# A planner's run-time order replaced by a table of issue order, engines and PSUM banks

## The chip, the cores and the metric

The kernel runs on one core of one Trainium2 chip. Its time is the device time of one execution in microseconds (us). Five queues of instructions work side by side and wait for each other through semaphores: TensorE (PE: matmuls; its weight loads are listed as PEld), VectorE (DVE), ScalarE (ACT), GpSimd (POOL) and SyncE (SP, which only issues DMAs here). Each executes in the order in which its instructions were written. Matmuls write into PSUM, eight banks of 128 x 2 KiB; DVE and ACT read it, POOL doesn't. A run counts as faster or slower here by the median of its times.

## The reference

Two layers follow each other. The first is an attention with a feature map of exponentials, for 8 batches, 8 heads, 576 tokens and 64 channels; the second is an MLP whose gate mixes the 576 tokens.

```python
def phi(x):                                  # x: 8, 8, 576, 64; w_phi: 64, 128
    proj = np.einsum('bhsd,df->bhsf', x, w_phi)
    proj = proj - np.max(np.abs(proj), axis=-1, keepdims=True)
    return np.concatenate([np.exp(proj), np.exp(-proj)], axis=-1)
q_p, k_p = (phi(q), phi(k))
kv = np.einsum('bhsf,bhsd->bhfd', k_p, v)
num = np.einsum('bhsf,bhfd->bhsd', q_p, kv)
den = np.einsum('bhsf,bhf->bhs', q_p, k_p.sum(axis=2))[..., None] + 1e-06
x = (num / den) with the heads side by side  # 8, 576, 512
h = np.maximum(x @ w_in, 0.0)                # w_in: 512, 1024
u, v = h[..., :512], h[..., 512:]
v_n = (v - mean(v)) / np.sqrt(var(v) + 1e-06)
v_s = np.einsum('ts,bsd->btd', w_spatial, v_n) + b_spatial[None, :, None]
out = (u * v_s) @ w_out                      # 8, 576, 512, float32
```

## The kernel before

**Tiles.** Of each batch's 576 tokens 512 are the main part (128 partitions, each with 4 tokens) and 64 are the tail; the tails of two batches share the 128 partitions. Attention works on *units*: a pair of heads of one batch (32 of them) or the tails of two batches with all heads (4). Main matmul operands are bf16, sums are float32 in PSUM.

**A unit** takes these steps, each an operation of the plan: q and k are transposed (early on PE with a copy out of PSUM, L630 and L636, from batch 2 on by a DMA transpose, L650); k is projected (L692); DVE takes the largest absolute value (`mk`, L719), ACT the two exponentials (`kf`, L728), and of the negated maxima (`em`, L735); POOL scales v by them (`vs`, L745 and L750). For q the maximum (`mq`, L795) is split into two bf16 parts (`mhl`, L806 and L811; on DVE for the first `EARLY` units, later on POOL), transposed by PE (L818), copied (`mT`, L824) and subtracted inside the projection (L834 and L839) before the exponentials (`qf`, L850). Then come the products with v (L899 and L902), their copy (`kv`, L911), the numerator (L927; tails L986), its division (L870 and L874 on DVE, into `x`), and the transpose of `x` for the MLP: a DMA transpose (L945) from unit `XX` on, PE with a copy before (L956, L962).

**The MLP of a batch**: four V products (L1031) with their ReLU into `vr` (L1020 or L1022), their mean and variance on DVE (L1046, L1048), the inverse root on POOL (`root`, L1057 to L1059), the normalized rows `vn` (L1064, POOL or DVE); four U products (L1158) with a ReLU into `uT`; four spatial products S (L1208, L1210) that DVE multiplies into `uT` (L1217); four output products O (L1101), each copied from PSUM to `ob` (L1106, ACT or DVE) and stored by SP (L1109). Tails take the same steps with half-size tiles (L1184, L1228, L1230, L1239).

**Constants.** `w_spatial` lies in a `vn` slot until PE has transposed it into `w_spT`, in six blocks of 576 columns. The last two hold the tail's 64 rows of either batch, with the bias as one more row. For them `f_bias` copies the tail columns and the bias into zeroed tiles `wspr` and `wsptr` (L576 to L579, eight copies), which PE transposes (L599, L600); L603 copies each block out of PSUM. All six block transposes wait for `f_bias`.

**What sets the order.** The kernel first lists its operations by calls of `add`: name, engines that may run it with a cost on each, what it depends on, a priority (a due time), buffers and PSUM banks that it takes. `Plan.order` then plays a schedule through with these costs: at each step the engine that can start first takes the ready operation of the earliest due time, an operation that two engines may do goes to the one that ends it first, banks are given out as they come free, and gaps of PE are filled with dummy matmuls (`keep_busy`, L402) up to a certain time. The operations are emitted in the order of the planned starts, and each engine keeps it. `SLOTS` has the number of buffers of each kind, `OFF`, `MLP` and `TUNE` the due times. A buffer kind with n slots goes round: the (n+1)-th use waits for the first one's readers.

Of the kernel before, what the change touches and what calls it, by code (L numbers as in the profile page):

```python
# [15 lines left out]
SLOTS = dict(kh=2, qh=3, vh=2, tl=1, kT=3, qT=7, kTb=1, qTb=3, kf=4, kft=2, qf=3, qft=2, vs=2, kv=3, x=3, xt=5,  # L16
             xT=3, xTt=3, vn=4, uT=2, uTt=1, vr=6, ob=7, mk=5, mq=2, em=3, emt=4, p0=4, mhl=1, mT=2)
OFF = dict(load=-24.36, T=-3.87, KP=-4.21, KM=0.82, KE=-8.23, EM=0.69, VS=-1.33, QP=0.79, QM=-5.85, MH=-0.05,
           MT=-3.88, FP=7.29, FE=8.25, KV=5.67, NU=8.31, XT=10.0)
PERIOD = 5.47  # L20
MLP = dict(at0=6.87, step0=1.63, at1=14.14, step1=1.44, at2=11.57, step2=1.84, at3=6.46, step3=1.72, at4=25.75,
           step4=0.83, at5=6.71, step5=1.58, at6=23.42, step6=0.25, at7=-1.6, step7=5.16)
TUNE = dict(lq=3.79, w0=-3.66, w1=-2.36, w2=6.25, w3=10.12, l8=-6.73, l9=4.4, l10=0.1, l11=-7.8, l13=0.92,
            tq=-2.75, tk=-9.53, vt0=4.02, vt1=-0.82, u8=-2.33, u9=3.32, u10=7.42, u11=0.12, u12=1.18, u13=0.32,
            u14=0.0, u15=0.76, u16=1.44, u17=0.87, u18=0.31, u19=-3.88, u20=-2.72, u21=-1.32, u22=-0.19, u23=0.75,
            u24=0.04, u25=-0.04, u26=1.88, u27=-4.23, u28=1.49, u29=-0.34, u30=-3.18, u31=-1.7, u32=-1.2, u33=1.1,
            u34=0.77, u35=1.94, v0=0.75, bsp=-10.97, WT=26.11, wsp=9.28, wstep=2.27, vload=-1.26, cross=30.56,
            KC=1.58, u0=0.3, u1=3.71, u2=5.78, u3=-5.24, u4=1.74, u5=-11.18, u6=4.58, u7=-2.79, l0=-3.51, l1=2.4,
            l2=-1.13, l3=-2.83, l4=3.99, l5=2.31, l6=11.26, l7=-3.04, T0=-20.55, XTp=15.35, TN=-1.21)
# [4 lines left out]
WARM = 62.86  # L34
WARM0 = 22.63
FILL = 0.54
EARLY = 10
TCA = 14
VG0 = -1
VG1 = 1  # L40
VG2 = 2
VG3 = 2
VGT = -1
XB = 2
XX = 7
# [4 lines left out]
LONE = 0.0  # L50
# [10 lines left out]
class Op:  # L61
    __slots__ = ("engs", "emit", "deps", "left", "nexts", "allocs", "uses", "prio", "mode", "work", "ready", "done",
                 "name", "eng", "start", "follow", "after", "banks", "gates", "last")
# [11 lines left out]
class Plan:  # L75
# [28 lines left out]
    def order(self):  # L104
        lanes = {"SW": [], "HW": []}

        def lane(e):
            return lanes["SW" if e == "POOL" else "HW"]

        free = dict.fromkeys(self.ENGS, 0.0)  # L110
        pools = {k: [0.0] * n for k, n in SLOTS.items()}
        banks = [0.0] * BANKS
        held = float("inf")

        def place(n, t):

            fit = [i for i in range(BANKS - n + 1) if max(banks[i:i + n]) <= t]
            if n == 1:
                return max(fit, key=lambda i: (banks[i ^ 1] == held, banks[i]))
            return max(fit, key=lambda i: (i % 2 == 0, min(banks[i:i + n])))  # L120
        cand = {e: [] for e in self.ENGS}
        mode, server, out = 0, 0.0, []

        def release(op):
            op.after = {e: max([op.ready] + [d.done + (OWN if d.eng == e else WAKE) for d in op.deps]) for e in op.engs}
            for e in op.engs:
                cand[e].append(op)

        for op in self.ops:
            if op.left == 0:  # L130
                release(op)

        def earliest(op, e):
            t = max(free[e], op.after[e])
            need = {}
            if op.banks:
                n = len(op.banks)
                t = max(t, min(max(banks[i:i + n]) for i in range(BANKS - n + 1)))
                if t == held:
                    return None  # L140
            for b in op.allocs:
                need[b.pool] = need.get(b.pool, 0) + 1
            for p, n in need.items():
                if len(pools[p]) < n:
                    return None
                t = max(t, heapq.nsmallest(n, pools[p])[-1])
            for b in op.uses:
                if b.at is not None and b.who not in (None, e):
                    t = max(t, b.end + WAKE)
            if op.work is not None and len(lane(e)) >= 8:  # L150
                t = max(t, lane(e)[-8])
            if e == "PE" and op.mode != mode:
                t = max(t, free[e] + SWITCH)
            return t

        todo = len(self.ops)
        while todo:
            best = None
            for e in self.ENGS:
                if not cand[e]:  # L160
                    continue
                est = [(t, op) for op in cand[e] if (t := earliest(op, e)) is not None]
                if not est:
                    continue
                t0 = min(t for t, _ in est)
                if best is None or t0 < best[0]:
                    best = (t0, e, est)
            if best is None:
                raise RuntimeError("stuck: " + ", ".join(f"{o.name}" for e in self.ENGS for o in cand[e])[:800])
            t0, e, est = best  # L170
            slack = SWITCH + 1 if e == "PE" else 1
            est = [(t, op) for t, op in est if t <= t0 + slack]
            ready = [op.mode for _, op in est]

            def rank(op):
                if e != "PE" or op.mode == mode:
                    return op.prio
                return op.prio + GROUP + (LONE if op.mode == 1 and ready.count(1) < 2 else 0)
            pick = min((rank(op), k, t, op) for k, (t, op) in enumerate(est))
            _, _, t, op = pick  # L180
            if len(op.engs) > 1:
                fin = {}
                for f in op.engs:
                    tf = earliest(op, f)
                    fin[f] = tf + op.engs[f][1] + BIAS.get(f, 0)
                g = min(fin, key=fin.get)
                if g != e:
                    e, t = g, earliest(op, g)
            cost, lat = op.engs[e]
            for f in op.engs:  # L190
                cand[f].remove(op)
            op.eng, op.start = e, t
            if e == "PE" and self.filler is not None and self.filler[0].done is not None:
                a = max(free["PE"], self.filler[0].done + WAKE) + (SWITCH if mode else 0.0)
                z = t - (SWITCH if op.mode else 0.0)
                pace = 55.6 if a > 1e3 * WARM0 else 106.7
                n = int((z - a) * (1.0 if a < 1e3 * WARM0 else FILL) / pace)
                fit = [i for i in range(BANKS) if banks[i] <= a]
                if n >= 3 and a < 1e3 * WARM and fit:
# [5 lines left out]
            if e == "PE":  # L205
                mode = op.mode
# [1097 lines left out]
```

## Time and profile before

| | us |
|---|---|
| median of three runs | 268.99 (267.04 to 269.32) |
| the profiled execution | 265.37 |
| its span, first to last instruction | 263.6 |
| PE busy, with its waits inside a pipelined run | 243.6 |
| DVE, ACT, POOL busy | 212.2, 205.8, 181.6 |

The durations below come from the profiled execution. In a line of a group the numbers after the bar are the group's busy time, the mean of one in ns, and the idle time before it with what ended it. A stretch lists the busy time of PE, PEld, DVE, ACT and POOL in it, then the granted clock of PE, the DMA share and GB/s. In the chain a row has its start, its length and what it was. A DMA's landing is told from its issue. Matmuls overlap, so a row of one is longer than the distance to the next.

### The profile page before, as it was taken

To read this page: it belongs to the slowest core of one execution; us is meant where nothing else is said; L and a number is where in the kernel's file an instruction comes from. 1 tells how busy PE (TensorE), PEld (TensorE's weight loads), DVE (VectorE), ACT (ScalarE), POOL (GpSimd) and SP (SyncE) were. 2 spreads that over 40 slices of the span, in tenths; PEclk is the share of its full clock that TensorE was granted. 3 is DMA by queue.
4 is the path that set the end of the run, shared out by engine and by line. 5 is a ranking of instruction groups with operands and counts; after the bars stand their busy time and mean duration, and the time that the engine had idled before them with its cause. 6 is when DMAs were issued, how large, how long until landed. Compare 5 with 4: busy or idle time off the path is not lost.

```text
span 263.6 us, 8301 instructions
## 1 busy us (share of the span) xinstructions
PE 243.6 (92%) x3331; PEld 151.1 (57%) x3331; DVE 212.2 (81%) x406; ACT 205.8 (78%) x341; POOL 181.6 (69%) x306
## 2 busy tenths in 40 slices
PE   6777879999999999989999999969999999999993
PEld 5555666665656656555565775535676665545451
DVE  6899999989988999898999988857988973646610
ACT  5899898879898959869989886938988887665043
POOL 8798949769997889668999958548997440173000
PEclk9999999999999999999999999999999999999999
DMA  7999996999599999998989999999754038320036
GB/s 140 209 235 202 229 210 69 230 162 130 51 211 211 228 161 198 181 280 83 185 108 169 160 166 178 211 276 232 125 122 82 16 28 211 112 80 1 0 116 246
DMA packets 85047, 41.12 MB, mean 156 GB/s; under 512 B 53968, under 2 KB 80272, under 8 KB 85008
## 3 DMA queue, kind: packets, MB, share of 16 engines
q1 hardware_dynamic: 58288, 29.14, 56.9%
q0 software_dynamic: 26640, 11.41, 36.2%
q8 instruction: 26, 0.43, 0.8%
q14 instruction: 13, 0.11, 0.1%
q10 hardware_dynamic: 80, 0.03, 0.0%
HBM read 32.85 MB, written 9.44 MB: 160 GB/s over the span
## 4 chain that ended last, share of the span: by engine, by line
PE 65%; DMA 14%; DVE 7%; POOL 5%; ACT 4%; issue 3%; DVEq 0%; ACTq 0%; POOLq 0%
PE banks L1101 11%; PE banks L1208 10%; PE banks L1158 9%; PE banks L1031 9%; DMA qh<-in_q_dram 7%; DMA w_in<-in_moe_w_in_dram 5%; PE banks L899 5%; PE banks L927 4%; PE banks L692 4%; PE banks L834 2%; PE banks L1210 2%; DMA kTb<-kh 2%; PE banks L839 2%; POOL vs L750 2%; DVE x L874 2%
## 5 line engine op out<-in xcount | busy, mean ns | idle before, releaser
L850 ACT ACTIVATE qf<-banks 128x1024 bf16<-128x1024 f32 x64 | 64.3, 1032 | 8.4 <-PE banks L839 8.4
L728 ACT ACTIVATE kf<-banks 128x1024 bf16<-128x1024 f32 (+1 forms) x66 | 65.6, 1010 | 4.6 <-PE banks L692 2.6
L750 POOL TENSOR_TENSOR vs<-vh,em 128x512 bf16<-128x512 f32 x64 | 65.5, 1044 | 0.5
L719 DVE TENSOR_REDUCE mk<-banks 128x8 f32<-128x1024 f32 x36 | 43.7, 1216 | 6.0 <-PE banks L692 4.6
L795 DVE TENSOR_REDUCE mq<-banks 128x8 f32<-128x1024 f32 x26 | 31.4, 1218 | 5.3 <-PE banks L692 4.3
L1208 PE MATMUL banks<-w_spT,vn 128*128 128x512 bf16 x128 | 32.9, 379 | 0.7 <-DVE x L874 0.7
L1031 PE MATMUL banks<-w_in,xT 128*128 128x512 bf16 x128 | 31.6, 379 | 0.0
L1101 PE MATMUL banks<-w_out,uT 128*128 128x512 bf16 x128 | 31.1, 379 | 0.0
L1106 ACT COPY ob<-banks 128x512 f32<-128x512 f32 (+1 forms) x28 | 16.4, 588 | 18.7 <-PE banks L1101 18.6
L1158 PE MATMUL banks<-xT,w_in 128*128 128x512 bf16 x128 | 31.0, 379 | 0.0
L1046 DVE BATCH_NORM_STATS2 stats<-vr 128x6 f32<-128x512 bf16 (+1 forms) x37 | 25.1, 680 | 5.3 <-ACT vr L1022 5.1
L899 PE MATMUL banks<-vs,kf 128*128 128x66 bf16 x512 | 24.7, 193 | 1.5 <-POOL vs L750 0.9
L1217 DVE TENSOR_TENSOR uT<-banks,uT 128x512 bf16<-128x512 f32 x32 | 21.6, 684 | 4.5 <-PE banks L1210 4.0
L899 PEld LDWEIGHTS <-kf 128*128 128x128 bf16 x512 | 21.8, 97 | 5.3 <-issue 1.9
L874 DVE TENSOR_TENSOR x<-banks,rc 128x512 bf16<-128x512 f32 x32 | 22.0, 688 | 0.7
L1064 POOL TENSOR_SCALAR vn<-vr,rs 128x512 bf16<-128x512 bf16 x29 | 22.2, 779 | 0.4
L1022 ACT ACTIVATE uT<-banks 128x512 bf16<-128x512 f32 x25 | 14.9, 603 | 8.6 <-PE banks L1158 8.6
L927 PEld LDWEIGHTS <-qf 128*128 128x128 bf16 x512 | 19.3, 97 | 4.1 <-issue 0.5
L927 PE MATMUL banks<-kv,qf 128*128 128x66 bf16 x512 | 21.2, 193 | 0.5 <-ACT kv L911 0.3
L902 PE MATMUL banks<-vst,kft 128*128 128x66 bf16 x128 | 21.1, 192 | 0.0
L1022 ACT ACTIVATE vr<-banks 128x512 bf16<-128x512 f32 x25 | 15.0, 605 | 5.9 <-PE banks L1031 5.3
L1208 PEld LDWEIGHTS <-vn 128*128 128x128 bf16 x128 | 11.6, 97 | 13.1 <-issue 0.3
(131 smaller groups left out, 490.0 us busy)
## 6 DMA issues: line engine op xcount, KB each, us to landing
out_dram<-ob SPq DMA_DIRECT2D x32, 256.0 KB, 3.5
vh<-in_v_dram SPq DMA_DIRECT2D x14, 512.0 KB, 6.6
kh<-in_k_dram POOLq DMA_DIRECT2D x15, 256.0 KB, 5.8
qh<-in_q_dram POOLq DMA_DIRECT2D x15, 256.0 KB, 7.8
vh<-in_v_dram SPq DMA_DIRECT2D x4, 256.0 KB, 8.1
v_tl<-in_v_dram SPq DMA_DIRECT2D x8, 128.0 KB, 7.3
w_in<-in_moe_w_in_dram POOLq DMA_DIRECT2D x2, 512.0 KB, 14.5
out_dram<-ob SPq DMA_DIRECT2D x8, 128.0 KB, 2.7
```

The source lines that it names most:

```text
L719: nc.vector.tensor_reduce(out=mk.t[:, cols(rs)], in_=heads(ck, rs), axis=AX.X, op=ALU.max, apply_absolute_value=True)
L728: nc.scalar.activation(out=kfc.t[:, s, cols(rs), :], in_=heads(ck, rs), func=AF.Exp, bias=0.0, scale=sc)
L750: nc.gpsimd.tensor_tensor(out=vs.t[:, s, :, 0:D].rearrange("p (r x) d -> p r x d", r=2), in0=vc.t[:, lo:lo + H, :].rearrange("p (x r) d -> ...
L795: nc.vector.tensor_reduce(out=mq.t[:, cols(rs)], in_=heads(cq, rs), axis=AX.X, op=ALU.max, apply_absolute_value=True)
L850: nc.scalar.activation(out=qc.t[:, s, cols(rs)], in_=cf.t[:, rs].rearrange("p r (x t) -> p (r x) t", t=P), func=AF.Exp, bias=0.0, scale=sc)
L899: nc.tensor.matmul(out=pv[:, hh, s, :], lhsT=u["kf"].t[:, s, j, :], rhs=u["vs"].t[:, s, j, :], start=(n == 0), stop=False)
L927: nc.tensor.matmul(out=pn[:, hh, pos * DA:(pos + 1) * DA], lhsT=u["qf"].t[:, s, 4 * (pos // 2) + 2 * hh + pos % 2, :], rhs=kv["c"].t[:, 2 ...
L1022: nc.scalar.activation(out=out_, in_=in_, func=AF.Relu, bias=0.0, scale=1.0)
L1031: nc.tensor.matmul(out=pv[r], lhsT=lhs(kc), rhs=w_in_bf[:, kc, HALF:DFF], start=(kc == 0), stop=(kc == KC - 1))
L1101: nc.tensor.matmul(out=po[r], lhsT=lhs(dc), rhs=w_out_bf[:, dc, :], start=(dc == 0), stop=(dc == KC - 1))
L1158: nc.tensor.matmul(out=pu, lhsT=w_in_bf[:, kc, dc * P:(dc + 1) * P], rhs=xT["c"].t[:, kc, :], start=(kc == 0), stop=(kc == KC - 1))
L1208: nc.tensor.matmul(out=ps, lhsT=VN[bb]["c"].t[:, sp, cs], rhs=w_spT[:, sp, 0:T0], start=(sp == 0), stop=False)
```

## The change

1. `Plan.order` no longer plans. It reads `ORDER`, a string of 1514 words. A number is the place of an operation in the list of `add` calls; a letter behind it is the engine (P, A, D, G, S for PE, ACT, DVE, POOL, SP) where more than one is allowed; the number behind a colon is the first PSUM bank. `w0x17` is 17 dummy matmuls into bank 0; there are 11 such words with 86 in all. The operations are emitted in the order of the words.
2. `SLOTS` changes: more of `qh`, `qTb`, `x`, `xT`, `mk`, `mq`, `em`, `emt`, `mT`; fewer of `qf`, `xTt`, `vn`, `ob`, `p0`. `EARLY` goes from 10 to 12, `TCA` (units whose transposed copies ACT may do) from 14 to 11, `XX` from 7 to 6. DMA transposes of q and k begin with the same unit as before.
3. `root` writes into the mean-and-variance tile itself: the variance plus 1e-6, then its power -0.5; the third operation (the negated mean) goes, and the normalization subtracts the mean and multiplies in place of adding and multiplying.
4. `wspr`, `wsptr` and their memsets go. `f_bias` only casts the bias to bf16, two copies on ACT. PE transposes the tail columns and the bias columns straight from where they were loaded, each of the last two blocks in ten transposes in place of five, and only these two wait for `f_bias`. The last block is copied out in two parts; the rows between are zeroed by one memset of `w_spT`'s last two blocks.
5. The last output block is copied in two halves of 256 columns, the first by ACT and stored from ACT's queue, the second by DVE and stored by SP.

```diff
+        out = []
+        for word in ORDER.split():
+            if word[0] == "w":
+                i, n = map(int, word[1:].split("x"))
+                op = Op("warm", {"PE": (n * 55.6, n * 55.6 + 164)}, lambda e, i=i, n=n: self.filler[1](i, n), 0.0)
...
+                head, _, bank = word.partition(":")
+                op = self.ops[int(head.rstrip("PADGS"))]
+                op.eng = dict(zip("PADGS", self.ENGS)).get(head[-1]) or next(iter(op.engs))
                 for k, b in enumerate(op.banks):
+                    b.at = int(bank) + k
             out.append(op)
...
+ORDER = """
+21 2 18 8D 3 9D 0 19 72 24 73 27 16 20 14 17 w0x17 117:2 11G 4 118D w0x4 125:6 23 5 6 7 189:4 22 26 126D 119:2
...
+1462 1469:4 1464 1471:1 1470 1477:6 1472 1480:4 1478D 1467:2 1479 1481D 1376 1370 1486:4 1468 1482 1465:3 1487A
+1488 1483:7 1466 1473:6 1484A 1485 1489:2 1474A 1476 1492:3 1490A 1475 1495:0 1491 1493A 1494 1498:6 1496A 1497
+1499 1500 1501 1502
+"""
...
     def f_bias(e):
         copy = nc.vector.tensor_copy if e == "DVE" else nc.scalar.copy
-        for bl, col in ((0, TL), (1, 0)):
-            copy(out=wspr[:, :, bl, bl * D:bl * D + TL], in_=wspc.t[:, :, T0:S])
-            copy(out=wsptr[:, bl, bl * D:bl * D + TL], in_=wspt[:, T0:S])
-            copy(out=wspr[:, :, bl, col:col + 1], in_=bsp.unsqueeze(2))
-            copy(out=wsptr[:, bl, col:col + 1], in_=bspt)
+        copy(out=bspb[:, 0:NB], in_=bsp)
+        copy(out=bspb[:TL, NB:NB + 1], in_=bspt)
...
+            r, rb = slice(bl * TL, (bl + 1) * TL), slice(TL - bl * TL, TL - bl * TL + 1)
+            for rr, main, tail in ((r, lambda cc: wspc.t[:, cc, T0:S], wspt[:, T0:S]),
+                                   (rb, lambda cc: bspb[:, cc:cc + 1], bspb[:TL, NB:NB + 1])):
                 for tp, cc in enumerate(POS):
+                    nc.tensor.transpose(out=pt[rr, tp * P:(tp + 1) * P], in_=main(cc), identity=ident)
+                nc.tensor.transpose(out=pt[rr, T0:S], in_=tail, identity=ident[:TL, :TL])
...
-            nc.gpsimd.tensor_scalar(out=var[r, 0:n], in0=m[r, 0:n, 1:2], scalar1=1e-6, scalar2=None, op0=ALU.add)
-            nc.gpsimd.tensor_scalar(out=rs[r, 0:n, 1:2], in0=m[r, 0:n, 0:1], scalar1=-1.0, scalar2=None, op0=ALU.mult)
-            nc.gpsimd.tensor_tensor(out=rs[r, 0:n, 0:1], in0=var[r, 0:n], in1=neghalf[r, 0:n].unsqueeze(2), op=ALU.pow)
+            d["rs"] = m = mv()
+            nc.gpsimd.tensor_scalar(out=m[r, 0:n, 1:2], in0=m[r, 0:n, 1:2], scalar1=1e-6, scalar2=None, op0=ALU.add)
+            nc.gpsimd.tensor_tensor(out=m[r, 0:n, 1:2], in0=m[r, 0:n, 1:2], in1=neghalf[r, 0:n].unsqueeze(2), op=ALU.pow)
...
+        if last:
+            h = DM // 2
+            for n, (e_, c, dma, cost) in enumerate((("ACT", act(h), nc.scalar, 600.0), ("DVE", dve(h), nc.sync, 480.0))):
+                cs = slice(n * h, (n + 1) * h)
...
+                    (nc.vector.tensor_copy if e == "DVE" else nc.scalar.copy)(out=ob.t[r, cs], in_=pc.t[r, cs])
...
+                    add("OD", {"ACT" if n == 0 else "SP": (cost, 0)}, lambda e, dst=dst, rr=rr, cs=cs, dma=dma: dma.dma_start(
+                        out=dst[:, cs], in_=ob.t[rr, cs]), prio - 20, deps=[o2], uses=bufs(ob), work=(900, 128 * 55 / 16))
```

The table was read by numbering the `add` calls. Against the order before, output blocks copied whole by DVE go from 9 to 16 (by ACT from 28 to 20), copies of transposed q and k on DVE from 18 to 21, one of the four `vst` memsets goes to POOL, and SP's first DMA is the first k load in place of `w_phi`. On POOL's queue the loads of q and k of batch 0 and of batch 1's first four heads stand ahead of all weights, and `w_in` stands behind those of batch 1's other heads.

## The prediction

> **What bounds the kernel now.** I read the busy shares first, then the stretches of 10 us, then the chain, the waits and the timeline around what the change touches.
>
> ```profile
> PE 243.6 (92%) x3331; PEld 151.1 (57%) x3331; DVE 212.2 (81%) x406; ACT 205.8 (78%) x341; POOL 181.6 (69%) x306
> ```
>
> TensorE (PE) looks full, but a busy PE may be a waiting one. So I also counted from the start of each matmul to the start of the next. Back to back, a 128x512 matmul takes 0.216 us in this trace (four in 0.86 in the chain), one of 128 columns 0.056, one of 66 columns 0.03. What exceeds that is stall: 38.5 us in all, 17.0 of it before 40 us, 2.4 from 40 to 50, 16.7 from 50 to 180, and 2.4 after that. A further 4.7 us went to 85 filler matmuls (L402), all before 26 us. So there are 43 us to win at the very most, and over half of that lies in the first 50.
>
> ```profile
> 10.00:20.00 10.00, 7.39 (x134) 5.56 (x134) 9.55 (x21) 9.28 (x17) 8.73 (x12) 1.00 1.29 230
> 20.00:30.00 10.00, 7.64 (x165) 5.89 (x160) 9.25 (x25) 8.52 (x16) 8.95 (x13) 1.00 1.26 212
> 40.00:50.00 10.00, 9.42 (x161) 6.48 (x160) 9.87 (x23) 8.47 (x17) 9.71 (x14) 1.00 0.87 146
> ...
> 200.00:210.00 10.00, 10.00 (x153) 6.34 (x152) 9.08 (x16) 7.76 (x14) 4.49 (x10) 1.00 0.22 42
> ```
>
> Columns: PE, PEld, DVE, ACT, POOL busy, clock, DMA, GB/s. From 10 to 60 us VectorE (DVE) is busy for 47.1 of 50 us while PE stalls: DVE paces the start. From 180 on PE runs without stall, so the end is the time at which that stretch begins, plus fixed work. The chain names another suspect for the start, the loads:
>
> ```profile
> 7.39 13.05 DMA w_in<-in_moe_w_in_dram
> 20.72 17.49 DMA qh<-in_q_dram
> ```
>
> The second half of `w_in` and other weights stand in the queue ahead of batch 1's q and k; that q load was issued at 20.7 and landed at 38.2. PE itself shows only 0.8 us of idle for it, so I count DVE as the limit and the loads as close behind.
>
> **The change part by part**, against this execution's own 265.4 us (span 263.6 and 1.8 around it). That is 3.6 below the 269.0 median of the other runs; I carry the difference over.
>
> *Bias block.* The eight copies of `f_bias` stand in DVE's queue at the worst place:
>
> ```profile
> 25.26 1.03 DVE L577 COPY wsptr<-wspt 64x64 bf16<-64x64 bf16 x1
> ...
> 27.54 0.14 DVE L806 CAST mhl<-banks 128x8 bf16<-128x8 f32 x1
> 27.72 0.17 DVE L811 TENSOR_TENSOR mhl<-banks,mhl 128x8 bf16<-128x8 f32 x1
> ```
>
> ```profile
> 27.94 0.38 PE L630 MATMUL banks<-ident,kh 128*128 128x128 bf16 x4 [1.01 <-DVE mhl L811]
> ```
>
> They run from 24.95 to 27.62, 2.7 us, and PE is idle for 1.0 behind them. After the change two small ScalarE copies replace them (0.2 to 0.3 each, by the small rows 0.226 of `em` and 0.292 of `wphi`). Added: a memset of 1152 bf16 per partition, about 0.55 by the `wspr` row (0.485 for 512 words), in place of 0.65, both in DVE's idle first 5 us; one more eviction into `w_spT`, 0.44; and ten more PE transposes, 20 against 10, at 0.056: +0.6 on PE.
>
> *DVE's queue.* I added row means for what stands ahead of the numerator product (L874) in the old order and in the table. Ahead of batch 0's last pair it is 40.6 us before and 35.9 after; of batch 1's, 61.9 and 57.4; of batch 4's, 151.8 and 147.5; of batch 5's, 173.1 and 170.3; of batch 7's, 218.7 and 218.2. Neighbours overlap (all rows sum to 233.5, the busy time is 212.2), so 4.5 is 4.1 of real time. This holds the bias block, three more transposed copies on DVE (0.42 each), two more units whose maxima are split on DVE (four ops of 0.154, taken from POOL), and some work put later. The table also gives seven more whole output copies to DVE (16 against 9, 0.69 each), most of them late, where DVE is half idle. With DVE 94% busy up to 60 us, at most 4.1 is gained and at least 0, if its waits for data grow instead; I take **-3.0**, nearer to the top because the busy share is near one.
>
> *Order of loads.* SP's first load, k, moves ahead of `w_phi`: issue at 0.72 in place of 1.36, **-0.6**, since the first cast and transpose wait for it (the trace has 0.8 of DVE idle there). On POOL's queue q and k of batch 0 and of batch 1's first four heads go ahead of all weights, those of its other heads ahead of `w_in`, and the first half of `w_in` moves from the 10th place to the 32nd, behind 16 DMA issues (8 before) and 13 value products and casts. Nearest rows: PE idle for q and k loads 0.8 and 0.6. I take **-0.8**; the ends are the losing rival below (+7.9) and the winning one (-8).
>
> *Table and buffers from 50 us on.* The PE work of the MLP that stands ahead of each pair's numerator differs by at most 3 us up to batch 5 (54.6 and 54.6 at pair 2 of batch 4), so the mixture is the old one. What differs is detail: banks, neighbours, engines, more `mT`, `mq`, `em`, `x` and `xT` slots, fewer `qf` and `ob`. PE's idle time behind the maxima chain (L818 and L630 waiting for `mhl`) is 4.2 us in all, 1.0 of it the bias block's. I take a third of the rest, **-1.0**; the ends are a loss of 3 and a gain of 4 (a quarter of the 16.7).
>
> *One more unit transposed by DMA:* four PE transposes fewer, -0.2, against +0.6 above: **+0.4**.
>
> *Root in two GpSimd ops:* `rs` L1058 goes, 0.24 times 13 on POOL. In the last batch it stands on the way to `vn`, but PE is busy with other products there (10.00 of 10 from 230 to 250): 0. Were that cover gone, 0.2.
>
> *Last block in two halves.* Now: copy 0.58, then issue at 259.86 and landing at 262.29. A half is 0.39 on ScalarE or 0.42 on DVE by the `kv` rows of 264 columns. Side by side they would win 0.16. But both read one bank, and this trace shows two engines waiting for each other over a bank without sharing data:
>
> ```profile
> DVE mk L719 <- ACT kf L728: 0.5, 2, 0.3
> ```
>
> ```profile
> ACT kf L728 <- DVE mk L719: 1.4, 3, 0.6
> ```
>
> So one half after the other: 0.81, +0.2; half the bytes may return 0.1: **+0.1**. The Trainium skill (PSUM — Partial Sum Buffer, "PSUM bank collisions raise a hardware error") says that two engines reading one bank and quadrant at once is an error even at different columns, and has it guarded by a semaphore; it speaks against this edit, and the two waits agree. Without that rule the edit would be -0.2.
>
> Sum: -3.0 -0.6 -0.8 -1.0 +0.4 +0.1 = **-4.9**: 260.5 for a profiled execution, **264** as a median. A stall that goes from the start isn't lost later, since PE's work from 180 us on stays in order and without gaps: after the last pair's numerator the table leaves 30 us of PE work where the old order leaves 34. DVE and PE are late next, together.
>
> **Rivals.**
> 1. *The weights come late (slower).* Ahead of the first half of `w_in` on POOL now stand 16 DMA issues of 0.75 us (12.0), 8 value products of 1.05 and 5 casts of 0.21 (9.4) and some 1.5 of setup, and POOL idled 3.4 in its first 20 us: issue at about 26 in place of 7.4. At 13 to 18 us to landing, as here, that is 39 to 44, and the first product that needs it starts at 39.6 now: a stall of 0 to 4.5. The other half follows some 7 us later, landing at 46 to 51; the first U product, which the table puts about 6 us earlier than today's 53.6, waits 0 to 3.4 more. Together up to +7.9, less the 4.9 won elsewhere: +3, **272**. It decides from a landing after about 44.5, 4.9 beyond today's start of that product. Against it: less is queued ahead when q and k of batch 1 are through early. Chance 0.13, other losses of a fixed order included.
> 2. *Nothing much changes.* DVE's earlier work only moves its waits; PE's stalls from 50 to 180 stay, and the extra output copies sit in DVE's way. Bias block's 1.0 and the first load's 0.6, less 0.5: about -1, **268**. Chance 0.17; this is also what is left if the table reproduces the old order in effect.
> 3. *The loads were the limit.* The chain holds 30 us of DMA before 38 us. If q and k of batch 1, no longer queued behind `w_in` and `w_out`, let PE fill half of the 17 us of stall before 40: -8, plus -1 each of table and bias: about -10, **259**. For it: the chain; against it: DVE's 94%. Chance 0.24.
>
> My forecast has the remaining 0.46. The range goes from 257.5, which leaves out the upper part of the third rival (0.07), to 270.5, which leaves out most of the first and the rim of the second (0.14): with that 0.79 is inside. About 1% is what a measurement of this kernel can tell from no change (266.3 to 271.7). Faster: 0.46 and 0.24 make 0.70; same 0.17; slower 0.13.
>
> **What would show it.** No `wsptr` rows on DVE, and no PE idle on `mhl` near 28 us. PE stall before 50 us down from 19.4 to about 15, the fillers about the same 86. DVE still above 9.2 of 10 from 10 to 60 us; if it falls below 8.5 while PE gains, the third rival holds. The first V product (L1031) near 36 us; a wait of it on DMA `w_in` means the first. PE from 180 on without stall. In the last 5 us an ACT and a DVE copy of 256 columns one after the other. I am wrong if stall between 50 and 180 us grows by more than 4, or if gains come from there and not from the start.

## The result and the profile after

| | before | after |
|---|---|---|
| median | 268.01 us (264.78 to 269.32, four runs) | 307.8 us (306.57 to 308.57, four runs) |
| ratio, 95% interval | | 1.157 (1.146 to 1.168) |
| the profiled execution, its span | 265.37, 263.6 | 308.57, 306.8 |

The ratios and their intervals, here and below, leave out the runs that took over 1.5% longer than the fastest of the same kernel; medians and ranges are of all runs.

The forecast was 264. The kernel is 16% slower, 37 us beyond the upper end of the range. The answers to the views shown of before follow. First the busy time of each engine over the span, then the chain's shares by engine, both from the page of after:

```profile
PE 251.7 (82%) x3301; PEld 155.3 (51%) x3338; DVE 216.9 (71%) x411; ACT 199.2 (65%) x332; POOL 229.1 (75%) x291
...
PE 37%; POOL 32%; DMA 10%; DVE 10%; issue 6%; ACT 1%; POOLq 1%; SPq 1%; DVEq 0%; ACTq 0%
```

PE isn't busy for 55.1 us (306.8 less 251.7), where it was 20.0 before: 35.1 of the 43.2 us that the span grew. The other 8.1 are busy time of PE: matmul rows are longer on average (S, 0.413 us in place of 0.379), and the granted clock is below 1.00 in many stretches now. GpSimd (POOL) has 47.5 us more work with 15 instructions fewer, and from 5% of the chain it came to 32%.

The stretches of after (columns: PE, PEld, DVE, ACT, POOL busy, clock, DMA, GB/s):

```profile
10.00:20.00 10.00, 8.13 (x142) 6.84 (x139) 9.07 (x20) 9.66 (x20) 7.16 (x12) 1.00 1.20 187
20.00:30.00 10.00, 6.48 (x115) 5.36 (x114) 5.85 (x15) 6.11 (x12) 6.12 (x8) 0.83 0.46 63
...
60.00:70.00 10.00, 5.28 (x77) 2.98 (x75) 7.06 (x12) 8.71 (x17) 9.68 (x8) 0.94 1.30 155
...
100.00:110.00 10.00, 5.41 (x94) 3.62 (x94) 5.65 (x9) 7.41 (x12) 9.63 (x8) 0.99 0.90 171
...
230.00:240.00 10.00, 3.75 (x33) 1.89 (x33) 3.94 (x5) 4.23 (x7) 9.89 (x10) 0.81 0.29 68
```

In three of them POOL is full, with 8 to 10 instructions in 10 us, while PE works for 3.8 to 5.4. In each of them a batch's four rows `vn` are normalized. What PE waited for (us in all, times, the longest):

```profile
PE banks L1174 <- POOL vn L1015: 12.1, 7, 4.6
PE banks L771 <- POOL mhl L764: 9.7, 3, 6.2
PE banks L852 <- POOL vs L703: 7.5, 5, 3.4
PE banks L855 <- POOL vst L728: 3.5, 1, 3.5
```

All listed waits of PE that POOL ended make 38.5 us, against 3.3 before. The second and third row are not the normalization itself but what stands behind it on POOL: the split maxima `mhl` and the scaled v, both of the attention. POOL's groups name the operation (busy, mean ns of one, idle before):

```profile
L1015 POOL TENSOR_SCALAR vn<-vr,mv 128x512 bf16<-128x512 bf16 x30 | 62.2, 2080 | 0.6
L1015 POOL TENSOR_SCALAR vnt<-vr,mv_t 64x512 bf16<-64x512 bf16 x7 | 14.6, 2084 | 0.6
...
L1015 DVE TENSOR_SCALAR vn<-vr,mv 128x512 bf16<-128x512 bf16 x2 | 0.8, 408 | 0.3 <-POOL mv L1010 0.3
```

The same group on POOL before:

```profile
L1064 POOL TENSOR_SCALAR vn<-vr,rs 128x512 bf16<-128x512 bf16 x29 | 22.2, 779 | 0.4
```

One normalization on POOL takes 2.08 us in place of 0.78, on the same tile with the same types: 37 of them (36 before) at 1.30 more are 48.1 us; POOL's busy time grew by 47.5. On DVE the same line still takes 0.41. The timeline of POOL in after shows what that does to its queue (start, duration):

```profile
101.95 8.26 POOL L1015 TENSOR_SCALAR vn<-vr,mv 128x512 bf16<-128x512 bf16 x4
110.16 0.19 POOL L759 CAST mhl<-mq 128x8 bf16<-128x8 f32 x1
110.43 0.20 POOL L764 TENSOR_TENSOR mhl<-mq,mhl 128x8 bf16<-128x8 f32 x1
```

Two ops of 0.2 us for the next unit's maximum stand behind 8.26 us of normalization. Here PE waited for `vn` itself (3.1 and 1.5 us). PE's longest wait for `mhl` comes at a later batch, where one of the two small ops stands behind the fourth row (POOL's timeline, then PE's):

```profile
237.55 2.07 POOL L1015 TENSOR_SCALAR vn<-vr,mv 128x512 bf16<-128x512 bf16 x1
239.59 0.20 POOL L764 TENSOR_TENSOR mhl<-mq,mhl 128x8 bf16<-128x8 f32 x1
```

```profile
239.85 0.29 PE L771 MATMUL banks<-ident,mhl 128*128 128x128 bf16 x1 [6.20 <-POOL mhl L764]
```

In the last microseconds of after the two halves of the last block stand one after the other (the number in brackets is the idle time before):

```profile
301.97 0.37 ACT L1063 COPY ob<-banks 128x256 f32<-128x256 f32 x1 [0.28 <-PE banks L1052]
...
302.38 0.42 DVE L1063 COPY ob<-banks 128x256 f32<-128x256 f32 x1 [4.94 <-ACT ob L1063]
```

### The profile page after: what moved, and what is told of

Read it like the earlier page. It is cut to its first block, busy times and chain, and to the rows that moved or that the text cites. A ratio compares the mean times of both kernels' runs of the same rounds, so it can differ in the third digit from the quotient of the medians.

```text
span 306.8 us, 8238 instructions
## 1 busy us (share of the span) xinstructions
PE 251.7 (82%) x3301; PEld 155.3 (51%) x3338; DVE 216.9 (71%) x411; ACT 199.2 (65%) x332; POOL 229.1 (75%) x291
## 4 chain that ended last, share of the span: by engine, by line
PE 37%; POOL 32%; DMA 10%; DVE 10%; issue 6%; ACT 1%; POOLq 1%; SPq 1%; DVEq 0%; ACTq 0%
POOL vn L1015 16%; PE banks L1052 8%; PE banks L1174 6%; POOL vs L703 6%; PE banks L984 5%; DMA v_tl<-in_v_dram 4%; POOL vnt L1015 3%; PE banks L645 3%; DMA kTb<-kh 3%; PE banks L1124 3%; DVE stats L999 2%; POOL mv L1010 2%; PE banks L880 2%; PE banks L852 2%; DMA vh<-in_v_dram 2%
## 5 line engine op out<-in xcount | busy, mean ns | idle before, releaser
L803 ACT ACTIVATE qf<-banks 128x1024 bf16<-128x1024 f32 x64 | 62.6, 1028 | 20.8 <-PE banks L792 17.7
L681 ACT ACTIVATE kf<-banks 128x1024 bf16<-128x1024 f32 (+1 forms) x66 | 64.1, 1005 | 13.9 <-DVE mk L672 7.8
L1015 POOL TENSOR_SCALAR vn<-vr,mv 128x512 bf16<-128x512 bf16 x30 | 62.2, 2080 | 0.6
L1174 PE MATMUL banks<-w_spT,vn 128*128 128x512 bf16 x122 | 36.9, 413 | 12.4 <-POOL vn L1015 12.1
L672 DVE TENSOR_REDUCE mk<-banks 128x8 f32<-128x1024 f32 x36 | 43.5, 1216 | 4.5 <-PE banks L645 3.9
L748 DVE TENSOR_REDUCE mq<-banks 128x8 f32<-128x1024 f32 x24 | 29.1, 1214 | 6.0 <-PE banks L645 5.9
L984 PE MATMUL banks<-w_in,xT 128*128 128x512 bf16 x118 | 29.8, 379 | 0.9 <-DVE ob L1072 0.2
L1072 ACT COPY ob<-banks 128x512 f32<-128x512 f32 (+1 forms) x20 | 11.7, 588 | 20.0 <-PE banks L1052 19.5
L880 PE MATMUL banks<-kv,qf 128*128 128x66 bf16 x512 | 22.3, 198 | 0.0
L698 POOL CAST vs<-em 128x32 bf16<-128x32 f32 x32 | 6.8, 215 | 19.3 <-PE banks L984 10.1
L864 ACT CAST kv<-banks 128x264 bf16<-128x264 f32 x25 | 9.6, 383 | 15.6 <-PE banks L855 14.7
```

Source lines behind the costliest of these rows:

```text
L672: nc.vector.tensor_reduce(out=mk.t[:, cols(rs)], in_=heads(ck, rs), axis=AX.X, op=ALU.max, apply_absolute_value=True)
L681: nc.scalar.activation(out=kfc.t[:, s, cols(rs), :], in_=heads(ck, rs), func=AF.Exp, bias=0.0, scale=sc)
L803: nc.scalar.activation(out=qc.t[:, s, cols(rs)], in_=cf.t[:, rs].rearrange("p r (x t) -> p (r x) t", t=P), func=AF.Exp, bias=0.0, scale=sc)
L880: nc.tensor.matmul(out=pn[:, hh, pos * DA:(pos + 1) * DA], lhsT=u["qf"].t[:, s, 4 * (pos // 2) + 2 * hh + pos % 2, :], rhs=kv["c"].t[:, 2 ...
L984: nc.tensor.matmul(out=pv[r], lhsT=lhs(kc), rhs=w_in_bf[:, kc, HALF:DFF], start=(kc == 0), stop=(kc == KC - 1))
L1015: (nc.vector if e == "DVE" else nc.gpsimd).tensor_scalar(out=dst, in0=src, scalar1=rs[:, 0:1], scalar2=rs[:, 1:2], op0=ALU.subtract, op1=A ...
```

## The experiments

Three theories stood at first. **Theory 1**: the normalization that subtracts costs more on POOL, and that alone makes the loss. **Theory 2**: the table itself is at fault (its order, fewer `vn` slots), and the long rows are its by-product. **Theory 3**: the place of the operands is at fault, since mean and root now lie in the tile that DVE wrote. Times are medians. The experiments ran in three groups, each on a chip of its own, and the kernel before was run beside them each time: 269.11 (19 runs), 268.71 (29) and 268.17 (17). Lines of the table in the diffs are cut out of its text.

### The ALU operation alone

The kernel after with one word changed. The mean is added in place of subtracted, so this kernel leaves out the mean's sign.

```diff
-                                                               op0=ALU.subtract, op1=ALU.mult)
+                                                               op0=ALU.add, op1=ALU.mult)
```

> The changed kernel with one word altered: the normalization adds the mean in place of subtracting it (so its output isn't the reference's: the sign of the mean is wrong). Theory 1: on GpSimd a tensor_scalar with subtract and mult takes 2.08 us where one with add and mult took 0.78, 37 times, and POOL's extra 48 us make the loss. Then the rows return to about 0.78 and the time falls to 258 to 266. Theory 2: the table itself is at fault (its order, fewer vn slots), the long rows are its by-product: the time stays above 295. Theory 3: the operands' place is at fault (mean and root now lie in the tile that DVE wrote): rows stay near 2.08 and the time near 308.

Measured: 270.39 (265.4 to 272.11), 0.993 of before (0.985 to 1.000). The line's own view in this kernel (shortest, median, longest in ns; first and last start in us):

```profile
L1015 POOL TENSOR_SCALAR vn<-vr,mv x30: 757/766/899, 61.9 to 250.5; 128x512 bf16<-128x512 bf16 x30
```

Same order, same buffers, same operands, same places in the queue: 0.77 again, and 37 us are back. Theories 2 and 3 fall for the loss. The time is above the 258 to 266 that I expected: the loss is gone, and hardly a gain is left. The waits of PE that POOL ended fall from 38.5 to 7.2 us.

### The old root within the table

The kernel after with the three-op root and the normalization that multiplies and adds as before; it is also the base for what follows.

```diff
-            d["rs"] = m = mv()
-            nc.gpsimd.tensor_scalar(out=m[r, 0:n, 1:2], in0=m[r, 0:n, 1:2], scalar1=1e-6, scalar2=None, op0=ALU.add)
...
+            nc.gpsimd.tensor_scalar(out=rs[r, 0:n, 1:2], in0=m[r, 0:n, 0:1], scalar1=-1.0, scalar2=None, op0=ALU.mult)
...
-                                                               op0=ALU.subtract, op1=ALU.mult)
+                                                               op0=ALU.add, op1=ALU.mult)
```

> The changed kernel with the old root and normalization put back (three GpSimd ops, add and mult), all else as changed. Theory 1: within 1% of the run that only adds, since the third op is 0.24 us on POOL 13 times; 258 to 267, and against the kernel before the 4.9 us faster that I summed, if the rest of my working holds. Theory 2: above 295. Theory 3: 258 to 267 as well.

Measured: 268.95 (266.51 to 271.77), 0.999 of before (0.993 to 1.004). So all the rest of the change, which I had put at -4.9, comes out at nothing. The third op costs 13 times 0.24 on POOL, and nothing can be seen of it in the time: the kernel with two ops and an addition isn't distinguishable from this one.

### The new root in the old kernel

The kernel before with only the two-op root and the subtracting normalization; the planner plays its schedule through anew with the costs that the change gives (1400 in place of 1720 for a root).

```diff
-            nc.gpsimd.tensor_scalar(out=rs[r, 0:n, 1:2], in0=m[r, 0:n, 0:1], scalar1=-1.0, scalar2=None, op0=ALU.mult)
...
-                                                               op0=ALU.add, op1=ALU.mult)
+                                                               op0=ALU.subtract, op1=ALU.mult)
```

> The kernel before with only the new root and normalization (two ops, subtract and mult); its planner still counts 0.74 us for a normalization. Theory 1: rows of 2.08 us, POOL some 45 us busier, and 295 to 315 us. Theory 2: within 1% of the kernel before. Theory 3: as theory 1.

Measured: 321.71 (316.21 to 323.79, four runs), 47 to 55 more than before. The line's view:

```profile
L1062 POOL TENSOR_SCALAR vn<-vr,mv x29: 2062/2066/2216, 58.0 to 298.2; 128x512 bf16<-128x512 bf16 x29
```

It takes neither the table nor any other part of the change to get the slow rows, and the loss is greater here than with the table. The 36 rows account for 47 us of POOL's time; what makes the rest (the planner's new order, or a lower clock: 0.935 as a mean in the profile) was not taken apart.

### The subtraction in the second place

Is it the subtraction, or its place as the first of two operations? This kernel (on the best one below) multiplies first, then subtracts the mean times the root; that product is a third small op on POOL.

```diff
+            nc.gpsimd.tensor_tensor(out=m[r, 0:n, 0:1], in0=m[r, 0:n, 0:1], in1=m[r, 0:n, 1:2], op=ALU.mult)
...
-                                                               op0=ALU.add, op1=ALU.mult)
+                                                               op0=ALU.mult, op1=ALU.subtract)
```

> The table with both sets of moves, the normalization written as value times root, minus mean times root (mult, then subtract), the product of mean and root as a third GpSimd op. If any subtract makes the GpSimd tensor_scalar slow, its rows are near 2.08 us and the time is above 295; if only a subtract in the first place does, the rows are near 0.78 and the time is 263 to 267.

Measured: 308.22 (307.8 to 308.64, two runs), 1.152 of before (1.143 to 1.161), and 43 more than the same kernel with the old root and the addition (265.11 in this group).

```profile
L1013 POOL TENSOR_SCALAR vn<-vr,mv 128x512 bf16<-128x512 bf16 x30 | 62.1, 2074 | 0.6
```

2.07 in either place. So it is the subtraction on POOL. Why it is slow there, no run shows.

### Where the -4.9 went: the bias block

With the loss explained, the open question was why the rest gives nothing. First, the bias block put back into the kernel with the old root: eight copies on DVE at the bias's place in the table, five transposes per block, and the two memsets.

```diff
-        copy(out=bspb[:, 0:NB], in_=bsp)
-        copy(out=bspb[:TL, NB:NB + 1], in_=bspt)
-    i_bias = add("bias", {"ACT": (196, 340)}, f_bias, WT + 4, [l_bsp, l_bspt])
+        for bl, col in ((0, TL), (1, 0)):
+            copy(out=wspr[:, :, bl, bl * D:bl * D + TL], in_=wspc.t[:, :, T0:S])
...
+    i_bias = add("bias", {"DVE": (900, 980)}, f_bias, WT + 4,
...
```

> As the run with the old root and normalization in the table, and the bias block put back too: zeroed copies made by eight DVE copies in the place of the table's bias word, five PE transposes for each of the two blocks. If the bias block is worth what I summed (up to 2.7 us of DVE in the paced stretch, of 3.0), this is 1.5 to 3 us slower than that run; if DVE has slack in the table's start, it is within 1.

Measured: 272.41 (269.59 to 276.6), 1.011 of before (1.000 to 1.021). That is 3.4 more than the 268.95 without it, though with these spreads anything from about 0 to 6 would fit. And the trace doesn't put it on the block. In the table the eight copies stand at 48.1 us, not at 25, and take 0.8 us together, not 2.7. The copies of `wsptr` (kernel before, then this one):

```profile
L577 DVE COPY wsptr<-wspt x2: 1015/1022/1028, 25.3 to 26.5; 64x64 bf16<-64x64 bf16 x2
...
L534 DVE COPY wsptr<-wspt x2: 163/164/165, 48.3 to 48.7; 64x64 bf16<-64x64 bf16 x2
```

DVE's row just ahead of them starts at 47.01, where the same row of the base kernel starts at 44.68: 2.3 us of the difference are there before the first copy. The row behind them is 3.1 late, the next of its kind 2.1. In the profiles PE waits 5.3 us for `kTb` and 3.5 for `vst` in place of 4.2 and 3.0, and those are loads and transposes that the block doesn't touch. What the block's change is worth in the table this run doesn't show; its own work there is 0.8 us of DVE, besides the memsets at the start.

### A queue that stands on one load

In the kernel with the old root PE idles twice for 3 us, on `vst`, where it did not before, and on `kTb`, where it waited 2.3 before. The first is in its weakest stretch:

```profile
20.00:30.00 10.00, 7.12 (x105) 5.89 (x106) 5.33 (x16) 5.57 (x11) 7.23 (x11) 0.66 0.59 91
```

DVE works 5.33 of 10 here, where it worked 9.25 before. POOL's timeline shows where that starts:

```profile
11.35 0.21 POOL L698 CAST vs<-em 128x32 bf16<-128x32 f32 x1 [0.28 <-ACT em L688]
14.53 1.04 POOL L703 TENSOR_TENSOR vs<-vh,em 128x512 bf16<-128x512 f32 x1 [2.97 <-DMA vh<-in_v_dram]
```

The table lets POOL scale the *second* pair's v ahead of the first's. The second v load was issued at 8.20 and landed at 14.45; the first pair's v had landed at 7.54 and stood in line behind it. The tail's v, which the table loads after that on SP (issued at 9.32 where it was 3.97, landed at 19.88 where it was 12.07), comes last of all, and PE waits for its product (PE's timeline):

```profile
22.89 0.21 PE L855 MATMUL banks<-vst,kft 128*128 128x66 bf16 x1 [3.02 <-POOL vst L728]
```

In the next kernel five words of the start are moved: on SP the tail's v loads ahead of the second v load, on POOL the first pair's products ahead of the second's and batch 0's tail ahead of batch 1's, on PE one projection of k ahead of a transpose.

```diff
-w0x4 125:6 23 5 6 7 189:4 22 26 126D 119:2 190 74 229:6 25 120A 75 76 230 w0x3 199:2 191 77 31
+w0x4 23 5 6 7 189:4 125:6 22 26 126D 119:2 190 74 229:6 120A 75 76 230 w0x3 199:2 191 77 25 31
...
-131:3 196 232 202
+131:3 196 198 197 232 202
...
-211 w6x6 237:5 214 198 205 206:2 238 212 217 197 w7x3 133:7 207 136D w6x4 129:1 134D 216 239 240
+211 w6x6 237:5 214 205 206:2 238 212 217 w7x3 133:7 207 136D w6x4 129:1 134D 216 215 239 240
...
-248 241:4 215 221
+248 241:4 221
```

> The table with the old root and normalization (269.0), and five words of the start moved: on POOL the two v products of the first pair go ahead of those of the second, and the two v products of batch 0's tail ahead of batch 1's; on SP the two v tail loads go ahead of the second v load, which waits for a transpose; on PE the first k projection goes ahead of the third k transpose. Theory A: what the table loses is head-of-line waiting in its start (POOL idle 3.0 us before its first v product, PE idle 3.0 us on the tail's, DVE busy only 5.3 of 10 us from 20 to 30): then the hole at 20 to 23 us closes and it is 3 to 4 us faster than that run, 265 to 266. Theory B: the start is slack, since PE has MLP work to catch up with later: within 1 us.

Measured: 267.16 (264.27 to 268.94), 0.991 of before (0.987 to 0.995). The stretch:

```profile
20.00:30.00 10.00, 8.14 (x165) 6.67 (x163) 9.38 (x24) 9.36 (x15) 7.66 (x11) 1.00 0.86 151
```

DVE is at 9.38, PE at 8.14 and the clock at 1.00; the 3 us on `vst` are gone. Over 20 to 40 us DVE works 18.5 of 20; in four profiles with the old start (the base kernel, the last block whole, two slots for `kTb`, the addition) it works 14.3 to 15.8. The time falls by 1.8, less than the 3 to 4 expected. The 3.0 was a long case: PE's wait on `vst` is 3.0, 2.2, 1.3 and 1.3 us in those four profiles.

### A transpose that waits for its only buffer

The second idle spell, from the waits and the timeline of the kernel with the old root (two views):

```profile
PE banks L645 <- DMA kTb<-kh: 4.2, 2, 3.0
```

```profile
72.95 0.60 PE L645 MATMUL banks<-wphi,kTb 64*128 64x128 bf16 x8 [2.99 <-DMA kTb<-kh]
```

`kTb`, the target of k's DMA transposes, has one slot. The projections that read its former content start at 62.48, the next transpose into it was issued at 63.81, and it landed 9.1 us later. The next kernel gives it two, and moves that transpose (the second of batch 2) up behind the one before it on SP.

```diff
-SLOTS = dict(kh=2, qh=4, vh=2, tl=1, kT=3, qT=7, kTb=1, qTb=4,
+SLOTS = dict(kh=2, qh=4, vh=2, tl=1, kT=3, qT=7, kTb=2, qTb=4,
...
-1034 160 339:6
+1034 160 159 339:6
...
-371 159 1059:1
+371 1059:1
```

> The table with the old root and normalization, a second kTb slot, and the DMA transpose of k for batch 2's second half moved ahead in SP's queue. In the run without it, it is issued at 63.8 after the readers of the one slot, lands at 72.9, and PE idles 3.0 us for it. Theory A (single waits at the table's fixed order cost what they last): 2.5 to 3.5 us faster, 265.5 to 266.5. Theory B: within 1 us, a later wait takes its place (DMA queues are the most loaded there).

Measured: 267.28 (263.89 to 268.89), 0.993 of before (0.988 to 0.997). The transpose is now issued at 55.5, and PE's wait for `kTb` falls to 1.3 us:

```profile
PE banks L642 <- DMA kTb<-kh: 1.3, 1, 1.3
```

### Both

> Both sets of moves. Theory A: the two add up, 262 to 263.5, 2% faster than the kernel before. Theory B: 266 to 269.

> The table with both sets of moves once more, on the chip of these runs, to compare the first two with: 262.5 to 266, about 1.5% faster than the kernel before.

The second is the same kernel once more, on the chip of the third group. Measured: 264.56 (262.49 to 265.2), 0.985 of before (0.979 to 0.990), and 265.11 (262.18 to 267.79), 0.987 (0.978 to 0.995). The two sets of moves add up within the spread: 1.8 and 1.7 apart, 4.4 and 3.8 together against 268.95. The base kernel ran on another chip; by the ratios to before, which allow for that, it is 2.0 and 1.6 apart, 3.8 and 3.2 together, each with about 2 to either side. Stretches of the first:

```profile
20.00:30.00 10.00, 8.46 (x174) 7.13 (x169) 9.42 (x21) 9.30 (x15) 6.42 (x10) 1.00 0.81 154
...
70.00:80.00 10.00, 9.35 (x154) 5.93 (x152) 9.79 (x18) 9.53 (x16) 6.98 (x10) 1.00 1.30 162
```

Where PE worked 7.12 and 6.62 in these two stretches of the base kernel, it works 8.46 and 9.35. This is the fastest kernel here, 1.3 to 1.5% better than the one before.

### Three edits that were asked for by a doubt

**The last block whole.** The base kernel with the last block copied by ACT and stored by SP, as the other blocks are.

```diff
-1499 1500 1501 1502
+1499 1500
...
-                       bufs(UT[bb]["c"]), [(dst, slice(0, P))], last=bb == B - 1 and j == NB - 1)
+                       bufs(UT[bb]["c"]), [(dst, slice(0, P))], last=False)
```

> The table with the old root and normalization, the last output block copied whole by ScalarE and stored by SP, as before the change. From the last matmul's end to the span's end it was 4.4 us in the kernel before and 4.9 with the halves, one after the other on their bank; I had 0.1. So the tail row: 4.4 to 4.5; the time 0 to 0.5 us below the run with halves, which a median can't tell.

Measured: 268.44 (265.8 to 273.5) against 268.95: no difference. From the last matmul's end to the end of the span it is 4.8 us whole and 4.9 in halves. The whole copy:

```profile
260.99 0.58 ACT L1074 COPY ob<-banks 128x512 f32<-128x512 f32 x1 [0.28 <-PE banks L1054]
```

0.58 here, and 0.37 and 0.42 with 0.03 between them in halves: a copy longer by 0.24, which half as much to store does not win back.

**More dummy matmuls.** The granted clock was 0.66 from 10 to 20 us in one profile of the fastest kernel, so its 86 dummies were doubled (`w0x17` to `w0x34` and so on).

```diff
-21 2 18 8D 3 9D 0 19 72 24 73 27 16 20 14 17 w0x17 117:2 11G 4 118D w0x4 23
+21 2 18 8D 3 9D 0 19 72 24 73 27 16 20 14 17 w0x34 117:2 11G 4 118D w0x8 23
```

> The table with both sets of moves and twice the dummy matmuls in each of the eleven words (172 in place of 86). The profile of the run without has a granted clock of 0.66 from 10 to 20 us, the kernel before had 1.00 there. Theory A: the clock costs time at the start: the share returns to 1.00 and it is 1 to 2 us faster. Theory B: DVE and the loads pace the start, so PE's clock is covered: within 1 us, or up to 2 slower where the dummies delay a transpose.

Measured: 267.55 (264.53 to 272.54), 0.998 of before, 2.4 slower than the same kernel without them in the same group. The other profile of that kernel, without extra dummies, has the clock at 1.00 there:

```profile
10.00:20.00 10.00, 8.07 (x147) 7.04 (x148) 9.07 (x20) 9.77 (x17) 8.56 (x14) 1.00 1.25 187
```

So the low clock was that execution's, not the order's, and the added dummies gained nothing. In their own profile the clock is 1.00 from 10 to 20 and 0.66 from 50 to 60.

**The bias block in the old kernel.** Only part 4 of the change, with the planner.

```diff
-    i_bias = add("bias", {"DVE": (900, 980), "ACT": (1000, 1100)}, f_bias, WT + 4,
-                    [l_wsp, l_wspt, i_wspr, i_wsptr, l_bsp, l_bspt], uses=bufs(wspc))
+        copy(out=bspb[:, 0:NB], in_=bsp)
+        copy(out=bspb[:TL, NB:NB + 1], in_=bspt)
+    i_bias = add("bias", {"ACT": (196, 340)}, f_bias, WT + 4, [l_bsp, l_bspt])
```

> The kernel before, planner and all, with the bias block alone changed (two casts on ScalarE, transposes straight from the loaded tiles). The planner makes a new schedule. If the 3.4 us that the bias block was worth in the table is its own, 264.5 to 267.5; if it was worth that much only at its place in the table, or the new schedule loses it, within 1 us of the kernel before.

Measured: 273.23 (269.72 to 274.73), 1.017 of before (1.009 to 1.024): slower by 1 to 2%, against both of my expectations. The planner makes another order from the changed costs. Two of PE's waits in it:

```profile
PE banks L690 <- DMA kTb<-kh: 2.2, 1, 2.2
PE banks L1182 <- DVE mq L793: 2.0, 1, 2.0
```

The wait on `mq` isn't in the profile of before; the one on `kTb` is, with 2.3. Counted from start to start, PE's stall is 46.2 us where it was 38.5. Whether the new order alone makes the 5 us was not tried (it would need the old order written out with the new block), so neither this run nor the one in the table shows what the block is worth.

## Why the prediction was wrong, by its steps

**Root in two ops: the failed step.** I priced what goes (`rs`, 0.24 times 13) and put the sum at 0 because PE was covered. The same line of the change also turns the normalization's addition into a subtraction, and that I gave no price at all: I took "subtracts and multiplies in place of adding and multiplying" for the same operation. It went from 0.77 to 2.07 us, 37 times, +48 us on POOL, +37 on the kernel (307.8 against 270.39 with the addition; 43 for the subtraction in the second place). By my own method it was a new operation that the trace of before does not show, and should have been bounded from both sides. The nearest rows were those of POOL on 512 elements, 0.77 and 1.04, and even the dearer would have been +0.27 times 37, 10 us; the true size was outside anything that these rows bound. The Trainium skill (GPSIMD Engine Reference, 4.1 Engine selection) has GpSimd at roughly line rate on elementwise add, mul or max with one input; it doesn't name subtraction. The additions here (0.77) may pass for that; the subtractions (2.07) do not, and there the measurement decides.

**The cover.** I had named it: PE busy at 10.00 of 10 from 230 to 250, "were that cover gone, 0.2". For the stretch that I meant it largely held: before has the rows of the last two batches there (231 to 242); in after they start from 269.3 to 275.5 and from 284.5 to 286.8, where PE works 9.95 of 10 from 270 to 280 and 8.11 from 280 to 290. It was missing for batches ahead of them, which my step left out: PE works 5.28 of 10 from 60 to 70 and 3.75 from 230 to 240 of after. POOL at 69% of the span looked like an engine with room; but a batch's four rows stand in one piece, and PE waits for them (12.1 us) and for what stands behind them (`mhl` 9.7 us, `vs` 7.5).

For the other steps the kernel with the old root and the one with both waits removed are what to compare with.

**Bias block**, -1.0 in PE's idle and a part of the -3.0: open. No `wsptr` row on DVE and no PE idle on `mhl` near 28 us in after, as foretold. But the run with the block put back has it at 48 us, where it takes 0.8 of DVE, and is late by 2.3 before it: the 3.4 us of that run are not shown to be the block's. Alone under the planner it lost 5.1, in another order.

**DVE's queue**, -3.0: the lower bound came true as written, "at least 0, if its waits for data grow instead". DVE has some 4 us less work ahead of the numerator of batch 0's last pair, as summed, and yet that row (L874 of before) starts at 41.8 us in the base kernel where it started at 39.7. I took the nearer end by DVE's 94%, as if its share would stay; in the base kernel it works 42.6 of the 50 us from 10 to 60, 85%, because POOL stood on a load and DVE's inputs came late. With that wait gone it is 44.8 and 45.8 in the two profiles of the fastest kernel, still below my 9.2 of 10.

**Order of loads**, -0.8, with the weights as the losing rival: I weighed the wrong load. `w_in` did come late, its halves landing at 39.4 and 48.3 as worked out (39 to 44, 46 to 51), and no wait of PE on it is in the profile: the first product that needs it starts only at 43.5, not at 36. The load that hurt was the second v, on SP, with POOL's queue standing on it for 3.0 us; moving five words brought 1.8. The first k load did move up (issued at 0.72, landed at 3.48 in place of 4.94). I had compared how much stands ahead of each load in its queue, but not in what order the *users* of two loads stand.

**Table and buffers after 50 us**, -1.0, ends of -4 and +3: what I had not read off the slots is that `kTb` has one, and that the table issues a transpose whose landing takes 9.1 us only when it is free: 3.0 us of PE idle, and 1.7 of time for a second slot and an earlier issue. Before shows the same wait at 2.3.

**Last block in halves**, +0.1: right within what can be measured; one after the other, as foretold from the two engines' waits for one bank.

**Fillers** 86, as said. **The stall before 50 us**, to fall from 19.4 to 15: 19.7 in the base kernel; with both waits removed 18.2 and 16.9 in two profiles. The stall counted over the whole of the base kernel is 49.2, but 37 of its 3338 matmul records are missing, all 128x512 ones by their groups; at 0.216 each that is 8.0, so 41.2 against 38.5 before. By the same correction after has 80.1. There the sign that I had named for being wrong came: from 50 to 180 us the stall is 40.9 in after, of which at most 8.0 are missing records, where it was 16.7. And PE isn't without stall from 180 on.

**The sum.** With the normalization as it was and five words and a slot mended, the kernel takes 264.6 and 265.1, near my 264. That is no proof of the other terms, and in part luck: as handed over, they came to 0, and what the two sets of moves brought, some 3 to 4 us, was no term of mine. Nor do the profiles show a gain at the start: the last pair's numerator (L874 of before) starts at 228.9 and 228.2 us in the fastest kernel, where it was 225.8 in before. What follows it is shorter, 34.1 us in place of 37.8, near the 30 against 34 us of PE work that I had counted there without making a term of it. The profile of before is a fast one of its kernel (265.4 of a median near 269), so how the gain of the medians divides stays open. Rival 2 ("nothing much changes", 268) describes the base kernel best.

## What to carry to other kernels

A changed ALU operation on GpSimd is a new instruction: price it by a row of the same operation or measure it, however alike it looks in the code; a negated operand and an addition in place of a subtraction were worth some 40 us here. An engine at 70% is not free where its work comes in one piece ahead of short operations that others wait for: look at what stands behind it in its queue. A fixed order has its own waits; before crediting it with a gain, ask for each load and each single-slot buffer which instruction stands first in the queue of the engine that uses it.

## What was not expected of the hardware

- On GpSimd a `tensor_scalar` with a subtraction, in the first or the second place, takes 2.07 us on 512 bf16 elements, with multiplication and addition 0.77, on 64 partitions as on 128 (2.08 and 0.76). On VectorE it is 0.41 either way.
- On GpSimd a power of 128x4 elements by `tensor_tensor` takes 1.04 us (0.58 on 128x1), a product of the same size 0.20 and the `tensor_scalar` beside it 0.24: most of the root is the power.
- Two DVE copies of 64x64 bf16 (`wsptr`) took 1.02 us each in before, where POOL scaled v beside them from 23.21 to 28.46, and 0.16 with the block at 48 us, where POOL stood idle. Whether POOL is the cause no run tests.
- Granted clock: 0.72 from 70 to 80 us of after and 0.81 from 230 to 240, stretches in or behind which PE idles; yet the fastest kernel had 0.66 and 1.00 in the same stretch from 10 to 20 in two executions that differ by 0.7 us in all. Low clock and idle PE go together in these traces, but not always.
